# mLSTM cell and squared-ReLU FFN on one core: the front of the kernel laid in another order

## Chip, core and metric

One NeuronCore of a Trainium2 chip runs the whole kernel. The metric is the device time of one launch in microseconds (us). TensorE does the matrix products, VectorE and ScalarE (and GpSimd) the elementwise work, and the queue of SyncE (SP) issues nearly all DMAs. Each engine takes its instructions in order; engines wait for each other through semaphores.

## What is computed

```
# q, k, v, o_gate: (4, 8, 768, 40); i_gate, f_gate: (4, 8, 768)
for t in range(S):
    m_new = max(f[t] + m, i[t])
    C = exp(f[t] + m - m_new) * C + exp(i[t] - m_new) * outer(v[t], k[t])
    n = exp(f[t] + m - m_new) * n + exp(i[t] - m_new) * k[t]
    y[t] = sigmoid(o[t]) * (C @ q[t]) / max(abs(n @ q[t]), 1)
    m = m_new
x = y as (3072, 320)                  # 8 heads of 40 side by side
out = max(x @ w_in, 0) ** 2 @ w_out   # w_in (320, 2048), w_out (2048, 320), stored as 64-bit floats
```

## The kernel before

**Chunks.** The recurrence is done in chunks of 128 steps: 4 batches of 6 chunks, s = 0 to 23, all 8 heads of a chunk together. Two chunks make a group g of 256 tokens, on which the FFN works. A chunk passes through these helpers:

- The gates (`do_gates`, L251, VectorE): a max-plus scan along all 768 steps for m, and a masked sum for A, the log decay since the chunk's start. Both are 32 rows (batch and head) by 768. `turn_gates` (L263) transposes them on TensorE, and ScalarE makes the bias b_T and the factor eA_T of them.
- `transposes(s)` (L411) turns k and q into kT and qT, `scores(s)` (L422) multiplies them on TensorE.
- The decay matrix comes to the 128 partitions in one of two ways. For chunks 0 and 1, `spread_A` (L346) makes it on TensorE: one fp32 matmul of the identity with the causal mask `later` per bank (L354), and one matmul per head that selects the row of A (L358). For all later chunks A goes to memory (`a_rows`, L916) and comes back by a broadcast load, `load_A` (L337, tile A_bc, 512 KB); GpSimd puts the mask on it (`mask`, L364, L367).
- `weigh(s)` (L379) is one ScalarE exponential per head (L391), and `values(s)` (L398) on GpSimd makes the weighted values vw. `weighted(s)` (L434) multiplies scores and weights on VectorE.
- `attend(s)` (L446): on TensorE hi (queries with the state C, L453), dC (L460) and hp (this chunk's part, L467); on VectorE the decay of hi (L473) and the mask on dC (L478); on GpSimd the update of C (L481, L486).
- `normalise(s)` (L585) makes x on VectorE (L589 to L599), `turn_rows(s)` (L624) transposes it on TensorE (L629), and ScalarE copies it (L630).

**FFN.** A group has four quarters pp. `ffn1_main` (L640) is 8 matmuls 256 tokens wide (L651) into two PSUM banks; `ffn1_rest` (L657, L662) adds the last 64 of the 320 inputs, from the weights w_in2; `relu_half` and `square_half` follow on ScalarE. Everything is fp32; an fp32 matmul shows as two records in the profile.

**Weights.** w_in and w_out come as 64-bit words and are turned to fp32 on the chip, piece by piece (18 pieces; 0, 1, 3, 4, 5, 6, 8, 9 are w_in, 2 and 7 are w_in2, the rest w_out). `fetch` loads a piece into one of four raw buffers; `words` (L195) is two ScalarE instructions (L202, L204); `join` (L207) is three VectorE instructions (L213, L217, L218) and one add on GpSimd (L222), after which it fetches the piece four further on. `step` does words and join.

**Order.** The kernel is under a manual schedule: each engine runs its instructions in the order in which the program text issues them. The front is the list from L896 to L955; then a loop of u = 0 to 7 (L959) takes chunks 2 to 5 and the first FFN quarters, and a longer loop (L1031) takes the rest. `NEXT` (L958) says how many pieces are joined by the end of each u. `idle(n)` (L880) is n bf16 matmuls of zeros, 128x512, on TensorE. PSUM is in three pools: ps_at (3 banks), ps_h (3), ps_o (2). `mask(2)` stands on GpSimd ahead of the update of C by chunk 1 and of the later joins (L941, L942, L946).

Of the kernel before, what the change touches and what calls it, by code (L numbers as in the profile page):

```python
# [17 lines left out]
P = 128  # L18
# [11 lines left out]
def kernel(  # L30
# [60 lines left out]
    conv = brought.enter_context(tc.tile_pool(name="conv", bufs=2, side="right"))  # L91

# [18 lines left out]
    later = gates.tile([P, P], F32)  # L111

# [4 lines left out]
    def make_consts():  # L117
# [4 lines left out]
        for t in va_w:  # L122
# [4 lines left out]

        nc.gpsimd.memset(sel[:], 0.0)
        nc.gpsimd.affine_select(
            sel[:], sel[:], compare_op=ALU.not_equal, fill=1.0, base=0, pattern=[[-1, H], [0, P]], channel_multiplier=1,  # L130
        )

        nc.gpsimd.memset(later[:], 0.0)
        nc.gpsimd.affine_select(
            later[:], later[:], compare_op=ALU.is_ge, fill=-1e30, base=0, pattern=[[1, P]], channel_multiplier=-1,
# [111 lines left out]
    def load_gates():  # L247
        nc.sync.dma_start(f_sb[:], f_gate.rearrange("b h s -> (b h) s"))
        nc.scalar.dma_start(i_sb[:], i_gate.rearrange("b h s -> (b h) s"))

    def do_gates():  # L251
        nc.vector.tensor_tensor_scan(m_sb[:], f_sb[:], i_sb[:], -1e30, op0=ALU.add, op1=ALU.max)
        nc.vector.memset(f_sb[:, 0:1], 0.0)
        nc.vector.tensor_tensor(f_sb[:, 1:], f_sb[:, 1:], m_sb[:, : S - 1], op=ALU.add)
        nc.vector.tensor_tensor(f_sb[:, 1:], f_sb[:, 1:], m_sb[:, 1:], op=ALU.subtract)
        nc.vector.tensor_scalar_max(f_sb[:], f_sb[:], LOG_ZERO)
        nc.vector.tensor_tensor_scan(
            A_sb[:], keep[:].rearrange("p c t -> p (c t)"), f_sb[:], 0.0, op0=ALU.mult, op1=ALU.add,
        )
        nc.vector.tensor_tensor(i_sb[:], i_sb[:], m_sb[:], op=ALU.subtract)  # L260
        nc.vector.tensor_tensor(i_sb[:], i_sb[:], A_sb[:], op=ALU.subtract)

    def turn_gates():  # L263
        for src, dst in ((i_sb, b_T), (A_sb, eA_T)):
            tp = ps_o.tile([P, W], F32, name="tp", tag="o_ps")[:, : S // P * BH].rearrange("p (c r) -> p c r", r=BH)
            for c in range(NB):
                nc.tensor.transpose(tp[:, c, :], src[:, c * P : (c + 1) * P], ident[:BH, :BH])
            nc.scalar.activation(
                dst[:].rearrange("p b c h -> p c b h"), tp.rearrange("p c (b h) -> p c b h", b=B),
                AF.Copy if dst is b_T else AF.Exp,  # L270
            )
# [74 lines left out]
    def spread_A(s):  # L346

        b, c = divmod(s, NB)
        H2 = H // 2
        d = st.setdefault(s, {})  # L350
        d["A"] = []
        for i in range(2):
            A = ps_h.tile([P, H2, P], F32, name="A_ps", tag="h_ps")
            nc.tensor.matmul(  # L354
                A[:], lhsT=ident[:], rhs=later[:].unsqueeze(1).to_broadcast([P, H2, P]), start=True, stop=False,
            )
            for h in range(H2):
                nc.tensor.matmul(  # L358
                    A[:, h, :], lhsT=sel[:, i * H2 + h, :], rhs=A_sb[:, c * P : (c + 1) * P],
                    start=False, stop=(h == H2 - 1),  # L360
                )
            d["A"].append(A)
# [16 lines left out]
    def weigh(s, masked=False):  # L379
        b, c = divmod(s, NB)  # L380
        d = st[s]
        A, n = d["A"], H // len(d["A"])
        d["W"] = flat_c[:, H * P * (s % 2) : H * P * (s % 2 + 1)].rearrange("p (h t) -> p h t", t=P) if s < W_IN else A[0]
        if s < X_SQ:
            d["dec"] = prep.tile([P, H], F32, name="dec")
        if len(A) == 1 and not masked:
            mask(s)
        for i in range(len(A)):
            hh = slice(i * n, (i + 1) * n)
            for h in range(n):  # L390
                nc.scalar.activation(  # L391
                    d["W"][:, i * n + h, :], A[i][:, h, :], AF.Exp, bias=b_T[:, b, c, i * n + h : i * n + h + 1],
                )
            if s < X_SQ:
                nc.scalar.activation(d["dec"][:, hh], A[i][:, :, P - 1], AF.Exp)
        values(s)
# [14 lines left out]
    def transposes(s, o=(False, False)):  # L411
        d = st[s]
        kqT(s)
        for i, n in enumerate(("kT", "qT")):
# [5 lines left out]
            (nc.scalar.copy if i == 0 or s in (0, *range(2, 7)) else nc.vector.tensor_copy)(d[n], tp)  # L420
# [25 lines left out]
    def attend(s):  # L446
        b, c = divmod(s, NB)
        d = st[s]
        C = st.get("C")
        if c > 0:  # L450
            hi = ps_at.tile([P, H, D1], F32, name="hi", tag="at")
            for j in range(PR):
                nc.tensor.matmul(  # L453
                    hi[:, 2 * j : 2 * j + 2, :].rearrange("p h d -> p (h d)"), lhsT=d["qT"][:, j, :],
                    rhs=C[:, j].rearrange("p h d -> p (h d)"), start=True, stop=True,
                )
        if c + 1 < NB:
            dC = ps_at.tile([P, PR, 2, D1], F32, name="dC", tag="at")
# [6 lines left out]
        hp = d["hp"] = ps_at.tile([P, H, D1], F32, name="hp", tag="at")  # L465
        for h in range(H):
            nc.tensor.matmul(  # L467
                hp[:, h, :], lhsT=d["P"][h % 2][:, h // 2, :], rhs=d["va"][:, h, :], start=True, stop=True,
            )
        d["num"] = hp  # L470
        if c > 0:
            num = d["num"] = old.tile([P, H, D1], F32, name="num", bufs=1)
            nc.vector.tensor_tensor(  # L473
                num[:], hi[:], eA_T[:, b, c, :].unsqueeze(2).to_broadcast([P, H, D1]), op=ALU.mult,
            )
        if c + 1 < NB:
            Cn = old.tile([P, PR, 2, D1], F32, name="C_sb")
            nc.vector.tensor_tensor(Cn[:], dC[:], bdm[:], op=ALU.mult)  # L478
            if c > 0:
                Cd = old.tile([P, H, D1], F32, name="Cd", bufs=1)  # L480
                nc.gpsimd.tensor_tensor(  # L481
                    Cd[:], C[:].rearrange("p j i d -> p (j i) d"),
# [4 lines left out]
            st["C"] = Cn  # L487

# [96 lines left out]
    def normalise(s):  # L585
# [4 lines left out]
        dm = work.tile([P, H], F32, name="dm")  # L590
# [3 lines left out]

        x = d["x"] = work.tile([P, 3 * P], F32, name="x_sb")
        x3 = x[:, :DM].rearrange("p (h d) -> p h d", d=D)
        nc.vector.tensor_tensor(x3, num[:, :, :D], d["og"], op=ALU.mult)
        nc.vector.tensor_tensor(x3, x3, dm[:].unsqueeze(2).to_broadcast([P, H, D]), op=ALU.mult)
        nc.vector.tensor_copy(x[:, DM:], x[:, DM - KR : DM])  # L599

# [39 lines left out]
    def ffn1_main(g, pp):  # L640

        if pp == 0:
            new_g2(g)
        xT = st["xT", g]

        hs = [ps_h.tile([P, 2, WG], F32, name="h_ps") for _ in range(2)]
        for i in range(2):
            for n in range(2):
                fb = 4 * pp + 2 * n + i
                for a in range(2):  # L650
                    nc.tensor.matmul(  # L651
                        hs[i][:, n, :], lhsT=w_in[:, a, fb * P : (fb + 1) * P], rhs=xT[:, :, a, :],
                        start=(n == 0 and a == 0), stop=False,
# [242 lines left out]
    load_gates()  # L896
    load_part(0, 0)
    load_part(0, 1)
    fetch(2)
    make_consts()  # L900
    load_part(1, 0)
    load_part(1, 1)
    load_part(0, 2)
    fetch(1)
    load_o(0)
    load_o(1)
    load_part(1, 2)
# [3 lines left out]
    idle(4)  # L911
    scores(0)
    idle(3)
    do_gates()
    rounding.words()
    nc.scalar.dma_start(A_d[:, :], A_sb[:])  # L916
    spread_A(0)
    rounding.words()
    turn_gates()
    rounding.join()  # L920
    weigh(0)
    transposes(1, (False, True))
    spread_A(1)
    scores(1, (True, True))
    weigh(1)
    first.close()
    ffn = ctx.enter_context(tc.tile_pool(name="ffn", bufs=2))
# [218 lines left out]
```

## Time and profile before

| | us |
|---|---|
| Median of 3 runs (513.91 to 514.52) | 514.11 |
| Profiled execution, own time | 512.99 |
| Its span | 511.2 |
| TensorE busy in it | 502.6 |
| VectorE busy | 347.0 |
| ScalarE busy | 248.7 |
| GpSimd busy | 112.7 |
| Mean granted TensorE clock | 0.997 of full |

Times in a timeline count from the span's start. A line has the start, the length, the engine (PE is TensorE, DVE VectorE, ACT ScalarE, POOL GpSimd), the source line, the operation, output<-inputs by the program's names, the shape, the number of instructions put together in the line, and in brackets how long the engine was idle before and what ended that. Lengths of overlapping instructions add up to more than the distance of their starts, so a cost per instruction is better read from start to start. A busy TensorE isn't one at its peak.

### The profile page before, as it was taken

What the parts mean: (1) busy time and instruction counts of PE and PEld (TensorE: products, weight loads), DVE (VectorE), ACT (ScalarE), POOL (GpSimd) and SP (SyncE); (2) the same over time, 40 slices, a digit from 0 to 9 for tenths busy, and PEclk for the clock granted to TensorE, in tenths of its full rate; (3) what the DMA queues carried; (4) which work ended last, traced back from release to release, by engine and by line L of the source; (5) the groups of instructions that cost most, each with busy time, mean ns of one, the idle gap of its engine ahead of it and who ended that gap; (6) DMA issues with size and microseconds to landing.
All of it is one profiled execution on the core that took longest, in us unless ns stands there. A gap on an engine that the chain in (4) does not pass through costs nothing.

```text
span 511.2 us, 11842 instructions
## 1 busy us (share of the span) xinstructions
PE 502.6 (98%) x4648; PEld 460.9 (90%) x4649; DVE 347.0 (68%) x630; ACT 248.7 (49%) x492; POOL 112.7 (22%) x138
## 2 busy tenths in 40 slices
PE   9999999999999999999999999999999999999997
PEld 4878888787798999999999999999999999999997
DVE  8588966564879767667768777667768666644341
ACT  3768798654440650770660870560861650432400
POOL 3356733312022121112112130122112121020000
PEclk9998999999999999999999999999999999999999
DMA  9999899855675786675675786685655352100000
GB/s 191 207 237 220 246 234 207 135 121 106 115 168 98 167 159 128 153 161 115 158 151 113 172 158 117 161 165 101 165 122 116 94 120 79 46 10 25 0 27 27
DMA packets 238231, 67.63 MB, mean 132 GB/s; under 512 B 185600, under 2 KB 232704, under 8 KB 238176
## 3 DMA queue, kind: packets, MB, share of 16 engines
q1 hardware_dynamic: 238080, 66.68, 61.6%
q8 instruction: 37, 0.61, 0.5%
q10 hardware_dynamic: 96, 0.20, 0.1%
q14 instruction: 18, 0.15, 0.1%
HBM read 54.56 MB, written 17.86 MB: 142 GB/s over the span
## 4 chain that ended last, share of the span: by engine, by line
PE 85%; DVE 8%; ACT 2%; issue 2%; DMA 2%; SPq 1%; POOL 0%; DVEq 0%; POOLq 0%; ACTq 0%
PE h_ps L742 32%; PE h_ps L816 21%; PE h_ps L848 7%; PE h_ps L651 6%; PE tp L429 4%; PE h_ps L688 3%; PE numT L528 3%; PE numT L519 2%; PE h_ps L662 2%; DVE mag L217 2%; PE hp L467 1%; DMA A_bc<-a_rows 1%; PE A_ps L358 1%; PE dC L538 1%; ACT g_c L391 1%
## 5 line engine op out<-in xcount | busy, mean ns | idle before, releaser
L367 POOL TENSOR_SCALAR_AFFINE_SELECT A_bc<-A_bc 128x1024 f32<-128x1024 f32 x22 | 25.5, 1161 | 215.0 <-ACT kq L377 170.0
L742 PE MATMUL h_ps<-T,S 128*128 128x160 f32 x352 | 51.4, 299 | 0.0
L742 PE MATMUL h_ps<-w_out,g 128*128 128x160 f32 x336 | 49.2, 303 | 0.0
L742 PEld LDWEIGHTS h_ps<-T,S 128*128 128x128 f32 x352 | 49.0, 190 | 0.0
L377 ACT ACTIVATE kq<-A_bc 64x512 f32<-64x512 f32 x30 | 18.9, 630 | 61.1 <-DMA A_bc<-a_rows 60.8
L391 ACT ACTIVATE A_bc<-A_bc,b_T 128x128 f32<-128x128 f32 x144 | 44.3, 391 | 8.4 <-POOL A_bc L367 7.9
L742 PEld LDWEIGHTS h_ps<-w_out,g 128*128 128x128 f32 x336 | 46.1, 190 | 1.1
L651 PE MATMUL h_ps<-xT,w_in 128*128 128x256 f32 x192 | 44.5, 386 | 1.6 <-ACT xT L630 1.6
L651 PEld LDWEIGHTS h_ps<-xT,w_in 128*128 128x128 f32 x192 | 36.1, 193 | 7.3 <-ACT xT L630 2.0
L829 ACT COPY r_sb<-h_ps 128x512 f32<-128x512 f32 x18 | 10.5, 586 | 63.8 <-PE h_ps L816 63.8
L816 PE MATMUL h_ps<-xT,w_in 128*128 128x128 f32 x288 | 40.7, 284 | 0.4 <-ACT r_sb L829 0.4
L758 DVE TENSOR_TENSOR y_sb<-y_sb,h_ps 128x160 f32<-128x160 f32 x44 | 14.1, 320 | 36.7 <-PE h_ps L742 36.6
L816 PE MATMUL h_ps<-xs,w_in 128*128 128x128 f32 x288 | 38.0, 275 | 0.0
L816 PEld LDWEIGHTS h_ps<-xT,w_in 128*128 128x128 f32 x288 | 34.9, 191 | 3.4 <-ACT r_sb L829 0.6
L848 PE MATMUL h_ps<-xT,w_in 64*128 64x128 f32 x432 | 36.9, 280 | 0.0
L848 PEld LDWEIGHTS h_ps<-xT,w_in 64*128 64x128 f32 x432 | 33.4, 187 | 2.2
L816 PE MATMUL h_ps<-xs,WS 128*128 128x128 f32 x288 | 35.1, 275 | 0.0
L816 PEld LDWEIGHTS h_ps<-xs,w_in 128*128 128x128 f32 x288 | 35.1, 192 | 0.0
L816 PEld LDWEIGHTS h_ps<-xs,WS 128*128 128x128 f32 x288 | 33.6, 192 | 0.0
L545 DVE STREAM_TRANSPOSE tn<-numT 128x256 f32<-128x256 f32 x36 | 15.9, 449 | 21.2 <-PE numT L528 21.2
L853 DVE TENSOR_TENSOR r_sb<-r_sb,h_ps 128x512 f32<-128x512 f32 x18 | 12.4, 686 | 25.7 <-PE h_ps L848 25.6
L444 DVE TENSOR_TENSOR A_bc<-tp,A_bc 128x512 f32<-128x512 f32 x36 | 23.1, 684 | 9.5 <-PE tp L429 9.5
(168 smaller groups left out, 1069.9 us busy)
## 6 DMA issues: line engine op xcount, KB each, us to landing
A_bc<-a_rows SPq DMA_DIRECT2D x22, 512.0 KB, 4.6
raw<-in_moe_w_out_dram SPq DMA_DIRECT2D x8, 640.0 KB, 4.7
num_rows<-tn SPq DMA_DIRECT2D x18, 256.0 KB, 3.0
kq<-num_rows SPq DMA_DIRECT2D x72, 64.0 KB, 2.6
kqT<-kq_rows SPq DMA_DIRECT2D x34, 128.0 KB, 3.2
raw<-in_moe_w_in_dram SPq DMA_DIRECT2D x8, 512.0 KB, 5.9
kq<-in_k_dram SPq DMA_DIRECT2D x24, 160.0 KB, 4.9
va<-in_v_dram SPq DMA_DIRECT2D x24, 160.0 KB, 5.2
```

The costliest lines, as they stand in the source:

```text
L367: nc.gpsimd.affine_select(A[:], A[:], compare_op=ALU.is_ge, fill=-1e30, base=0, pattern=[[0, H], [1, P]], channel_multiplier=-1,)
L377: nc.scalar.activation(e[rows], st[s]["A"][0][rows, PR * i : PR * (i + 1), :], AF.Exp)
L391: nc.scalar.activation(d["W"][:, i * n + h, :], A[i][:, h, :], AF.Exp, bias=b_T[:, b, c, i * n + h : i * n + h + 1],)
L429: nc.tensor.matmul(sc[i][:, j, :], lhsT=d["kT"][rows, j, :], rhs=d["qT"][rows, j, :], start=True, stop=True,)
L444: nc.vector.tensor_tensor(t, d["sc"][i], d["W"][:, heads, :], op=ALU.mult)
L528: nc.tensor.matmul(numT[i][halves[g], e, :], lhsT=va_w[s % NKQ][:, h * D1 : h * D1 + DP], rhs=d["P"][h % 2][:, h // 2, :] if s < KQ_SQ els ...
L545: nc.vector.transpose(to[:, 2 * i : 2 * i + 2], numT[i][:, :2, :].rearrange("p c t -> p (c t)"))
L651: nc.tensor.matmul(hs[i][:, n, :], lhsT=w_in[:, a, fb * P : (fb + 1) * P], rhs=xT[:, :, a, :], start=(n == 0 and a == 0), stop=False,)
L688: nc.tensor.matmul(o_ps, lhsT=st["g2", g][:, fb, j * P : (j + 1) * P], rhs=w_out[:, fb, :], start=(fb == 0), stop=(fb == NF - 1),)
L742: nc.tensor.matmul(to, lhsT=lhsT[:, p], rhs=rhs[:, p, :], start=(start and p == 0), stop=(p == NPAIR - 1), skip_group_check=True,)
L816: nc.tensor.matmul(to[:, n, :], lhsT=lhsT[:, 4 * q + n, :], rhs=rhs, start=(start and n == 0), stop=True, skip_group_check=True,)
L848: nc.tensor.matmul(to[:, n, :], lhsT=w_in2[rows, 4 * q + n, :], rhs=rhs, start=False, stop=True, skip_group_check=True,)
```

## The change

- The gates are done in two parts: the first two chunks (256 steps), then the other four. Each part has its own loads (`load_gates(part)`), `gates_floor`, `gates_sum` and `turn_gates`. The arithmetic is reordered: f - i, plus the m before, clamped from both sides, gives the log decay, and its part above zero plus A gives minus b, whose sign the copy to b_T turns.
- `spread_A` is split: `spread_mask` puts the mask into both banks by bf16 matmuls (identity and mask are copied to bf16 on VectorE); bank i holds the heads of parity i.
- `weigh` can do the first or second half of its heads alone; `ffn1_main` can do one chunk (128 tokens) alone; `attend` is cut into `from_C`, `to_C`, `from_chunk`, `decayed`, `next_C`, and `normalise` into `denominators` and `gated`. Calls that aren't in the front keep the order within them, but hp's matmuls go even heads first.
- `transposes` copies both tiles on ScalarE (before, qT of chunk 1 went to VectorE).
- The order of loads: k and q of chunk 2 come into the first list, the values behind the keys and queries, raw pieces later.
- The front is in a new order, with fewer idle matmuls (15 of 27 remain). Chunk 2's scores, both halves of the first FFN quarter and the transposes of chunk 3 come before the loop. In the loop, u = 0 has chunk 3's weights only, and at u = 1 ffn1(0,1) stands ahead of attend(2); at u = 2 turn_rows(2) comes after ffn1(0,2).

The diff, cut; the bodies of `from_C` to `next_C` and of `denominators` and `gated` are those of `attend` and `normalise`:

```diff
+        nc.gpsimd.memset(later[:], 0.0)
+        nc.gpsimd.affine_select(
+            later[:], later[:], compare_op=ALU.is_ge, fill=-1e30, base=0, pattern=[[1, P]], channel_multiplier=-1,
+        )
+        nc.vector.tensor_copy(ident_h[:], ident[:])
+        nc.vector.tensor_copy(later_h[:], later[:])
...
+    FIRST = 2
+    SPANS = (slice(0, FIRST * P), slice(FIRST * P, S))
...
+    def gates_floor(part):
+        cols = SPANS[part]
+        c0, c1 = cols.start, cols.stop
+        tt = nc.vector.tensor_tensor
         nc.vector.tensor_tensor_scan(
+            m_sb[:, cols], f_sb[:, cols], i_sb[:, cols], -1e30 if c0 == 0 else m_sb[:, c0 - 1 : c0],
+            op0=ALU.add, op1=ALU.max,
         )
+        g = i_sb
+        tt(g[:, cols], f_sb[:, cols], i_sb[:, cols], op=ALU.subtract)
+        if c0 == 0:
+            nc.vector.memset(g[:, 0:1], 0.0)
+        a = max(c0, 1)
+        tt(g[:, a:c1], g[:, a:c1], m_sb[:, a - 1 : c1 - 1], op=ALU.add)
+        nc.vector.tensor_scalar(f_sb[:, cols], g[:, cols], scalar1=0.0, scalar2=LOG_ZERO, op0=ALU.min, op1=ALU.max)
+
+    def gates_sum(part):
+        cols = SPANS[part]
+        nc.vector.tensor_tensor_scan(
+            A_sb[:, cols], keep[:].rearrange("p c t -> p (c t)")[:, cols], f_sb[:, cols], 0.0, op0=ALU.mult, op1=ALU.add,
+        )
+        nc.vector.scalar_tensor_tensor(
+            i_sb[:, cols], in0=i_sb[:, cols], scalar=0.0, in1=A_sb[:, cols], op0=ALU.max, op1=ALU.add,
+        )
...
+    def spread_mask(s):
+
+        d = st.setdefault(s, {})
+        d["A"] = [ps_h.tile([P, PR, P], F32, name="A_ps", tag="h_ps") for _ in range(2)]
+        for A in d["A"]:
+            nc.tensor.matmul(
+                A[:], lhsT=ident_h[:], rhs=later_h[:].unsqueeze(1).to_broadcast([P, PR, P]), start=True, stop=False,
+            )
...
-    def weigh(s, masked=False):
+    def weigh(s, masked=False, part=None):
...
-            (nc.scalar.copy if i == 0 or s in (0, *range(2, 7)) else nc.vector.tensor_copy)(d[n], tp)
+            nc.scalar.copy(d[n], tp)
...
-    def ffn1_main(g, pp):
+    def ffn1_main(g, pp, half=None):
...
+        js = slice(0, GT) if half is None else slice(half, half + 1)
+        cols = slice(js.start * P, js.stop * P)
...
-                        hs[i][:, n, :], lhsT=w_in[:, a, fb * P : (fb + 1) * P], rhs=xT[:, :, a, :],
-                        start=(n == 0 and a == 0), stop=False,
+                        hs[i][:, n, cols], lhsT=w_in[:, a, fb * P : (fb + 1) * P], rhs=xT[:, js, a, :],
+                        start=(n == 0 and a == 0 and not half), stop=False,
...
-    load_gates()
+    load_gates(0)
     load_part(0, 0)
     load_part(0, 1)
-    fetch(2)
+    load_gates(1)
     make_consts()
+    load_part(0, 2)
     load_part(1, 0)
     load_part(1, 1)
-    load_part(0, 2)
     fetch(1)
     load_o(0)
+    load_part(1, 2)
+    fetch(1)
     load_o(1)
-    load_part(1, 2)
+    fetch(1)
+    load_part(2, 0)
+    load_part(2, 1)
     fetch(1)
     idle(12)
     transposes(0)
-    idle(4)
+    spread_mask(0)
+    idle(3)
+    gates_floor(0)
+    gates_sum(0)
+    spread_A(0, 0)
+    turn_gates(0)
+    spread_A(0, 1)
     scores(0)
-    idle(3)
-    do_gates()
+    weigh(0)
+    gates_floor(1)
+    weighted(0)
+    gates_sum(1)
     rounding.words()
+    transposes(1, (True, True))
+    spread_mask(1)
+    for i in range(2):
+        spread_A(1, i)
+    weigh(1, part=0)
     nc.scalar.dma_start(A_d[:, :], A_sb[:])
-    spread_A(0)
+    weigh(1, part=1)
+    rounding.join()
+    from_chunk(0)
+    to_C(0)
+    denominators(0)
+    next_C(0)
+    scores(1, (True, True))
     rounding.words()
-    turn_gates()
+    sigmoid(0)
+    sigmoid(1)
+    rounding.words()
     rounding.join()
-    weigh(0)
-    transposes(1, (False, True))
-    spread_A(1)
-    scores(1, (True, True))
-    weigh(1)
-    first.close()
-    ffn = ctx.enter_context(tc.tile_pool(name="ffn", bufs=2))
-    before = ExitStack()
-    old = before.enter_context(tc.tile_pool(name="old", bufs=2))
-    weighted(0)
     weighted(1)
-    load(2)
+    load_part(2, 2)
     load_A(2)
     load_o(2)
     load_o(3)
-    sigmoid(0)
-    sigmoid(1)
-    attend(0)
-    rounding.step()
-    normalise(0)
+    to_C(1)
+    from_C(1)
+    turn_gates(1)
+    first.close()
+    ffn = ctx.enter_context(tc.tile_pool(name="ffn", bufs=2))
+    from_chunk(1)
+    gated(0)
+    decayed(1)
+    turn_rows(0)
     mask(2)
-    attend(1)
+    transposes(2)
     normalise(1)
+    next_C(1)
+    ffn1_main(0, 0, 0)
+    rounding.words()
+    turn_rows(1)
     load(3)
     load_A(3)
-    rounding.step()
-    turn_rows(0)
-    idle(4)
-    transposes(2)
-    idle(4)
+    rounding.join()
+    rounding.words()
+    scores(2)
+    ffn1_main(0, 0, 1)
+    ffn1_rest(0, 0, st["half"][0])
+    rounding.join()
+    weigh(2, masked=True, part=0)
+    relu_half()
+    weigh(2, masked=True, part=1)
+    transposes(3, (True, True))
+    rounding.join()
+    weighted(2)
     sigmoid(2)
     sigmoid(3)
-    turn_rows(1)
-    weigh(2, masked=True)
-    rounding.step()
...
     for u in range(8):
         s = 2 + u // 2
         relu_half()
-        if u % 2 == 0:
-            if u == 0:
-                ffn1(0, 0)
-                scores(s)
-                rounding.step()
-            else:
+        if u == 0:
+            weigh(3)
+            rounding.words()
+            square_half()
+        elif u % 2 == 0:
+            if u > 2:
                 turn_rows(s - 1)
-                scores(s)
-                ffn1(u // 4, u % 4)
+            scores(s)
+            ffn1(u // 4, u % 4)
             if u == 2:
+                turn_rows(s - 1)
                 rounding.words()
             weighted(s)
...
+            if u == 1:
+                ffn1(0, 1)
             attend(s)
...
-            transposes(s + 1)
+            if u > 1:
+                transposes(s + 1)
             rounding.words()
-            ffn1(u // 4, u % 4)
+            if u > 1:
+                ffn1(u // 4, u % 4)
             square_half()
```

## The prediction

> **What bounds the kernel now.** I read first the page's busy shares, then the timelines of TensorE, GpSimd and VectorE over the first 70 us (the change ends there), then the DMA answer for the first 50 us.
>
> The page's first rows, engine busy shares and the forty slices:
> ```profile
> PE 502.6 (98%) x4648; PEld 460.9 (90%) x4649; DVE 347.0 (68%) x630; ACT 248.7 (49%) x492; POOL 112.7 (22%) x138
> PE   9999999999999999999999999999999999999997
> ```
> TensorE has no hole in any slice, so after the front a delay or a lead of TensorE is carried to the end. I therefore ask one thing: at what time does TensorE reach the first step that is the same in both kernels? That is turn_rows(3), the transposes of chunk 3's x, at 64.92 before.
>
> TensorE before, around the first FFN matmuls (start, length, instruction, wait):
> ```profile
> 27.23 0.82 PE L883 MATMUL idle<-zeros 128*128 128x512 bf16 x3
> 31.25 3.72 PE L651 MATMUL h_ps<-xT,w_in 128*128 128x256 f32 x16 [0.57 <-ACT xT L630]
> 34.90 1.14 PE L662 MATMUL h_ps<-xT,w_in 64*128 64x256 f32 x8
> 43.81 4.12 PE L651 MATMUL h_ps<-xT,w_in 128*128 128x256 f32 x16
> 50.49 3.72 PE L651 MATMUL h_ps<-xT,w_in 128*128 128x256 f32 x16
> 64.92 0.52 PE L629 MATMUL tp<-ident,x_sb 128*128 128x128 f32 x3 [0.52 <-DVE x_sb L598]
> ```
> The FFN quarters (0,0), (0,1), (0,2) start at 31.25, 43.81 and 50.49. At 64.92 TensorE waits for VectorE, so VectorE is level with it there.
>
> GpSimd before, in its program order:
> ```profile
> 27.96 1.35 POOL L367 TENSOR_SCALAR_AFFINE_SELECT A_bc<-A_bc 128x1024 f32<-128x1024 f32 x1 [2.84 <-DMA A_bc<-a_rows]
> 29.28 0.97 POOL L481 TENSOR_TENSOR Cd<-C_sb,dec 128x328 f32<-128x328 f32 x1
> 30.33 1.04 POOL L486 TENSOR_TENSOR C_sb<-C_sb,Cd 128x328 f32<-128x328 f32 x1
> 32.52 1.32 POOL L222 TENSOR_TENSOR w_in<-mag,low 128x512 int32<-128x512 int32 x1 [1.15 <-DVE mag L218]
> ```
> mask(2) cannot start before A_bc of chunk 2 lands (27.9); C's update and the weights' final add stand behind it.
>
> The DMA answer for 0 to 50 us:
> ```profile
> DMA  0499999999999989896989699999999689999996
> q1 hardware_dynamic: 27262, 10.39, 102.1%
> A_bc<-a_rows SPq DMA_DIRECT2D x3, 512.0 KB, 5.8
> ```
> From 3 us to 50 us SP's queue never runs dry: what lands when is set by the bytes queued ahead, not by when a load is asked for.
>
> **What the notes say.** (1) The Trainium skill, DMA: Bandwidth & Descriptors, Queues, rings and completion order: on each DMA engine descriptors are consumed in ring order. The trace agrees: loads land in the order of issue, 4.8 to 8 us after it. (2) The Trainium skill, GPSIMD Engine Reference, Specifications: GpSimd's SBUF interfaces are shared with VectorE, which contends when it has two SBUF inputs or runs a 2-port mode. The trace agrees: L217 takes 0.43 us alone (22.61) and 1.38 beside L222 (32.75). (3) The Trainium skill, TensorE: Matmul & The Clock Gate, Part 1: after an idle window of about 3.4 us the array runs at half rate. The trace is harsher: TensorE has nothing from about 38.0 to 39.1, and the windows show a granted clock of 0.50 at 42 to 44 us.
>
> **The change part by part.**
>
> *Gates in two parts.* VectorE before: 4.12 to 10.19 for A. A 768-wide scan takes 1.74, so 256 columns take (1.74-0.06)/3+0.06 = 0.62; a subtract or add 0.35, the clamp 0.22. Two scans, two tensor_tensor, a clamp: 2.3 us with gaps. VectorE is free at 3.9 (memsets to 3.50, two new copies to bf16 at an estimated 0.2). The loads of a third of the bytes are then there (whole ones: 3.7 and 4.1). A for chunks 0 and 1 is ready at 6.2, 4.0 us sooner.
>
> *Masks in bf16.* L354 takes 1.02 us per bank in fp32. The same shape in bf16 is L883: four from 28.76 to 29.71, 0.24 each. Four masks: 4 x 0.78 = 3.1 us off TensorE. Idle matmuls: 12 of 27 go, about 2.6 us. The price of the half-width FFN: eight 128-wide matmul records of L816 take 0.99, so 16 take 1.98, twice that is 3.96 against 3.65: +0.3.
>
> *ScalarE.* sigmoid(0,1) and sigmoid(2,3) are now split by exponentials: two more table loads of 1.28. The copy of chunk 1's qT moves to ScalarE (0.6). Cover: ScalarE is idle 3.45 us at 37.4 to 40.8 before.
>
> *The front's gain.* weigh(0) runs from 9.1 instead of 14.51: gates turned at 8.5, behind the idle(3) and one spread_A of 1.08. Then ScalarE: 2.2 for weigh(0), 1.15 words, 1.1 copies, 2.4 for weigh(1): done at 16.0 (20.6 before). VectorE: gates_floor(1), weighted(0), gates_sum(1) to 13.9; join of piece 0 to 15.5; then piece 1, which meets GpSimd's add of piece 0, to 19.1; weighted(1) to 20.4 (21.8 before). TensorE: hp(1) 20.9 to 22.6, turn_rows(0) to 23.1, transposes(2) to 24.1, the half FFN on chunk 0 24.1 to 26.1, turn_rows(1), scores(2), the half on chunk 1 27.7 to 29.7. Before, this work (L651 and scores(2)) is done at about 36.0. So at 29.7 TensorE leads by 6.3 us.
>
> *Where the lead ends.* The next step, ffn1_rest(0,0), needs piece 2 of the weights (w_in2), whose add on GpSimd is queued behind mask(2) and C's update, as before. But the load of A_bc(2) now stands behind one more transfer: raw piece 5, 512 KB, issued by the join of piece 1 ahead of it (before: raw 5 came after). At the rate of this stretch that is 1.6 us (2.15 between landings before). Nothing else ahead of it changes by more than a few tenths, so A_bc(2) lands at about 27.9+1.6-0.2 = 29.3, although its issue comes sooner. GpSimd sits idle from 20.4 to then. From there one chain, each link in program order on its engine:
> - mask, Cd, add: 3.4 (27.96 to 31.37): 32.7. Piece 2: 1.3: 34.0.
> - ffn1_rest 1.05: 35.1. relu_half stands between the halves of weigh(2) on ScalarE: 1.05 + 1.25: 37.4. vw(2) 0.8: 38.2. Piece 4, queued behind vw(2): 1.3: 39.5.
> - ffn1(0,1) 4.85, now ahead of attend(2): 44.3. hi(2) 0.95: 45.3.
> - VectorE has waited since 38.7 (weighted(2)): decay and C 1.4, join of piece 5 1.8, normalise(2) 2.7 with contention, join of piece 6 1.6: 52.8. Add on GpSimd 1.3: 54.1.
> - ffn1(0,2) starts at 54.1 (before 50.49) and takes 4.8; turn_rows(2) 0.5: 59.4. Attend(3) starts there, 55.21 before.
>
> The lead of 6.3 us has become a lag of 4.2. The words of piece 9 stand behind turn_rows(2)'s copy on ScalarE (60.1), so the join of piece 9, attend(3)'s VectorE part and the join of piece 10 follow: x of chunk 3 near 69.3, against 65.0: **+4.3 us**.
>
> *The clock.* TensorE stalls at 29.7 to 34, 36 to 39.5 and 49 to 54. One 1.1 us stall before cost a stretch of 3.4 us at half rate, 1.7 us of work. Bounds: 0 (the stretch falls into the next stall, and before has one too) to three hits, 1.05 for ffn1_rest and 1.7 each for (0,1) and (0,2): 4.5. I take one, **+1.7**.
>
> Sum against the profiled execution's own 512.99 (span 511.2 and 1.8 around it): 512.99+4.3+1.7 = 519.0. The median of the runs is 1.1 higher: 514.1+6.0 = **520.1**.
>
> **The rivals.**
> - *A_bc(2) lands early (not slower).* The chain above gives equality when ffn1(0,2) starts 0.5 before turn_rows(2)'s old place, that is when ffn1(0,1) starts at 36.9, so A_bc(2) at 26.7 decides. For it: A's write to memory is issued near 14.9 only, but its load right after join 1, and a transfer may overtake. Against: the full queue. At 24.5 the chain starts 4.8 sooner, the stalls shrink and no half clock comes (before pays about 1.3): 512.
> - *TensorE's work alone counts.* It is at 98%; 3.1+2.6-0.3 = 5.4 us less work would end at 508.7, if GpSimd and VectorE kept pace. Against it: VectorE would have to stand ready with pieces 5 to 7 at 45, with two holes of 7 us ahead.
> - *Every stall halves the clock.* +4.3+4.5: 522.9, up to 525 if A_bc(2) is later still.
> - *A wash.* Joins that fall into holes of GpSimd are 0.95 shorter (1.38 against 0.43 for L217). If four more than I allow are short and the clock holds: 514.1+4.3-3.8 = 514.6.
>
> **How the numbers follow.** A measurement of this kernel can tell about 0.2% (1 us) from no change. Forecast, 515.2 to 522: 0.50. Half clock at every stall, above 522: 0.17. Wash: 0.08. Early landing, 510.5 to 513: 0.13. TensorE's work alone, below 510.5: 0.12. Slower 0.67, same 0.08, faster 0.25. The range leaves out the lowest case and what lies above 524.5: 511.0 to 524.5. The forecast's own range is 515.2 to 522.
>
> **What would show it.** GpSimd idle for some 8 us ahead of mask(2), released by the DMA of A_bc near 29; TensorE waiting before L662's line for w_in2 on GpSimd; VectorE idle before hi(2) for over 4 us; ffn1(0,2) later than 50.5; a granted clock of 0.5 somewhere between 30 and 60 us. If mask(2) starts before 26.7, the prediction is wrong.

## The result, and the profile after

| | before | after |
|---|---|---|
| Median (before 513.91 to 514.52; after 528.71 to 530.68, 4 runs) | 514.26 | 529.12 |
| Ratio, 95% interval | | 1.0295 (1.0273 to 1.0317) |
| Profiled execution, its own time | 512.99 | 530.68 |
| Its span | 511.2 | 528.8 |
| Mean granted TensorE clock | 0.997 | 0.961 |

Slower, as forecast, but by 14.9 us where 6.0 were forecast, and above the range (511.0 to 524.5). Of some kernels below, one or two runs lie over 1.5% above the fastest; the ratios leave these out, the medians do not. The page of the kernel after, in its first rows and the row of granted clock:

```profile
PE 512.7 (97%) x4649; PEld 471.8 (89%) x4649; DVE 343.0 (65%) x636; ACT 250.8 (47%) x497; POOL 111.3 (21%) x138
PE   9997689999999999999999999999999999999997
...
PEclk9668697999999999999999999999999999999999
```

A slice is 13.2 us. TensorE now has holes in slices 4 to 6, as the chain of the prediction said, and five of the first seven slices show a clock below 9. Slice 2 (13 to 26 us) has a busy digit of 9 and a clock digit of 6: TensorE works without a pause and is slow. The same in stretches of 10 us, first before, then after; the third number from the right (PEclk) is the granted clock:

```profile
core 0: us, PE busy (x) PEld busy (x) DVE busy (x) ACT busy (x) POOL busy (x), PEclk, DMA share, GB/s
20.00:30.00 10.00, 9.95 (x84) 8.68 (x83) 8.73 (x21) 6.97 (x16) 4.06 (x4) 1.00 0.90 207
50.00:60.00 10.00, 10.00 (x78) 8.78 (x75) 9.79 (x14) 8.20 (x20) 6.54 (x7) 1.00 0.74 233
```
```profile
20.00:30.00 10.00, 10.00 (x57) 9.56 (x57) 4.63 (x10) 3.82 (x8) 2.44 (x3) 0.50 1.03 256
50.00:60.00 10.00, 6.50 (x56) 5.21 (x52) 7.62 (x16) 5.91 (x10) 3.24 (x5) 0.78 0.27 69
```

Both are fully busy from 20 to 30 us, but where before has 84 matmul records, after has 57 (not all of the same work), at a clock of 0.50. In stretches of 1 us the profiled run after is at half rate at 11.2 (for 3.4 us), 18.1 (17.1), 45.4 (3.4), 55.6 (10.2) and 79.5 (6.8): 41 us. Before has one stretch of 3.4 (both have some again in the last microsecond).

TensorE after, around the first FFN matmuls:

```profile
38.96 1.14 PE L719 MATMUL h_ps<-xT,w_in 64*128 64x256 f32 x8
44.46 4.98 PE L708 MATMUL h_ps<-xT,w_in 128*128 128x256 f32 x14 [2.90 <-POOL w_in L228]
61.14 5.60 PE L708 MATMUL h_ps<-xT,w_in 128*128 128x256 f32 x14 [3.34 <-POOL w_in L228]
80.10 0.87 PE L684 MATMUL tp<-ident,x_sb 128*128 128x128 f32 x3 [2.76 <-DVE x_sb L649]
```

ffn1_rest(0,0) starts at 38.96 (34.90 before), ffn1(0,1) waits for its weights until 44.46 (43.81), ffn1(0,2) until 61.14 (50.49), and turn_rows(3), where the prediction measured, is at 80.10 (64.92): 15.2 later, of the 17.7 by which this execution is longer. The rest comes just behind it, where the last stretch of half rate lies (79.5 to 86.3): turn_rows(4) is 18.1 later (98.42 for 80.29). ffn1_rest(0,0) isn't held by its weights here, whose add ends at 36.2; TensorE itself gets there only at 38.96. GpSimd and VectorE after:

```profile
28.83 1.09 POOL L396 TENSOR_SCALAR_AFFINE_SELECT A_bc<-A_bc 128x1024 f32<-128x1024 f32 x1 [5.51 <-DMA A_bc<-a_rows]
29.89 0.74 POOL L523 TENSOR_TENSOR Cd<-C_sb,dec 128x328 f32<-128x328 f32 x1
32.84 0.94 POOL L528 TENSOR_TENSOR C_sb<-C_sb,Cd 128x328 f32<-128x328 f32 x1 [2.21 <-DVE C_sb L520]
34.93 1.31 POOL L228 TENSOR_TENSOR w_in<-mag,low 128x512 int32<-128x512 int32 x1 [1.16 <-DVE mag L224]
```
```profile
30.02 0.50 DVE L638 TENSOR_TENSOR num<-num,hp 128x328 f32<-128x328 f32 x1 [4.06 <-PE hp L502]
32.20 0.49 DVE L520 TENSOR_TENSOR C_sb<-dC,bdm 128x328 f32<-128x328 f32 x1
51.58 0.50 DVE L511 TENSOR_TENSOR num<-hi,eA_T 128x328 f32<-128x328 f32 x1 [8.19 <-PE hi L481]
```

mask(2) is released by the load of A_bc at 28.8 after 5.5 us of idleness, as predicted (29.3). But behind it the add to C waits 2.2 us more for VectorE's masked dC (L520). On VectorE that stands behind normalise(1), which waits 4.1 us for hp(1) (L638), done only at 29.8 on a TensorE at half rate. The load was the last link in the plan; at half rate TensorE is.

### The profile page after: what moved, and what is told of

It is laid out like the page before. It is cut to its first block, busy times and chain, and to the rows that moved or that the text cites. A ratio compares the mean times of both kernels' runs of the same rounds, so it can differ in the third digit from the quotient of the medians.

```text
span 528.8 us, 11861 instructions
## 1 busy us (share of the span) xinstructions
PE 512.7 (97%) x4649; PEld 471.8 (89%) x4649; DVE 343.0 (65%) x636; ACT 250.8 (47%) x497; POOL 111.3 (21%) x138
## 4 chain that ended last, share of the span: by engine, by line
PE 89%; DVE 5%; issue 2%; POOL 1%; ACT 1%; DMA 1%; SPq 0%; POOLq 0%; DVEq 0%
PE h_ps L799 31%; PE h_ps L873 21%; PE h_ps L708 8%; PE h_ps L905 7%; PE tp L459 4%; PE numT L577 3%; PE h_ps L745 3%; PE h_ps L719 2%; PE numT L568 2%; PE hp L502 2%; PE dC L491 1%; DVE mag L223 1%; PE hi L481 1%; PE dC L587 1%; PE A_ps L388 1%
## 5 line engine op out<-in xcount | busy, mean ns | idle before, releaser
L708 PE MATMUL h_ps<-xT,w_in 128*128 128x256 f32 (+1 forms) x208 | 52.5, 412 | 8.6 <-POOL w_in L228 7.5
L708 PEld LDWEIGHTS h_ps<-xT,w_in 128*128 128x128 f32 x208 | 41.8, 221 | 16.7 <-POOL w_in L228 8.9
L815 DVE TENSOR_TENSOR y_sb<-y_sb,h_ps 128x160 f32<-128x160 f32 x44 | 14.0, 318 | 37.6 <-PE h_ps L799 37.6
L873 PEld LDWEIGHTS h_ps<-xT,w_in 128*128 128x128 f32 x288 | 34.9, 191 | 2.8 <-issue 0.5
L910 DVE TENSOR_TENSOR r_sb<-r_sb,h_ps 128x512 f32<-128x512 f32 x18 | 12.4, 687 | 25.7 <-PE h_ps L905 25.5
```

Of the source, the lines that this page charges most:

```text
L708: nc.tensor.matmul(hs[i][:, n, cols], lhsT=w_in[:, a, fb * P : (fb + 1) * P], rhs=xT[:, js, a, :], start=(n == 0 and a == 0 and not half), ...
L873: nc.tensor.matmul(to[:, n, :], lhsT=lhsT[:, 4 * q + n, :], rhs=rhs, start=(start and n == 0), stop=True, skip_group_check=True,)
```

## The experiments

Two theories. **Order**: the waits of the new order make up the loss, whatever the clock. **Clock**: a large part is TensorE at half rate, either because of its empty stretches or because of what it is given to do in the front. Where kernels of different groups are compared, it is by their ratios to the kernel before. Idle matmuls are zeros in bf16 whose product nobody reads; those in front of a mask are overwritten by it.

**1. Idle matmuls all through the new front; none at all in the old one.**

```diff
# after_warm: 33 more, idle(3) behind scores(0), spread_A(1, *), to_C(0), scores(1),
# from_C(1), from_chunk(1), transposes(2), and
     transposes(3, (True, True))
+    idle(12)
# before_cold: the three idle(4) of the front out
-    idle(4)
```

Expected of after_warm:

> The changed kernel with 33 more idle matmuls (seven groups of 3 in the front, 12 ahead of ffn1(0,1)). Clock theory (the thin matmuls and the missing fillers let the granted clock fall to half, and half-rate work on TensorE is most of the loss): the half-rate time falls from 34 to 41 us to under 14 us, hp(1) ends near 24 instead of 30, and the time is 516 to 521 us. Order theory (the waits of the new order on GpSimd and VectorE are the loss): the fillers add work, 528 to 533 us. A further point for either: with a full clock mask(2), released by A_bc at about 29, is the link that comes last ahead of the first ffn1_rest.

Expected of before_cold:

> The kernel before without its three idle(4) groups (one after transposes(0), two about transposes(2)); 12+3 idle matmuls remain, as in the changed kernel. Clock theory: half-rate stretches appear in the first 35 us, 517 to 523 us. Order theory: nothing was lost with them, 512 to 514.5 us.

after_warm 524.45, ratio 1.019 (1.0166 to 1.0215): about 5 us come back, with 20.5 us at half rate in the profiled run: between the two ranges, for more than the 14 us expected stay at half rate. before_cold 514.45, 0.9989 (0.9969 to 1.0009), no difference, where the clock theory asked for 517 to 523: it has 10 us at half rate and the time doesn't show it. So activity in the new front counts, and in the old front the idle matmuls are no gain or loss.

**2. The bf16 masks alone, in the kernel before.**

```diff
-                A[:], lhsT=ident[:], rhs=later[:].unsqueeze(1).to_broadcast([P, H2, P]),
+                A[:], lhsT=ident_h[:], rhs=later_h[:].unsqueeze(1).to_broadcast([P, H2, P]),
```

Expected of before_bf16:

> The kernel before with the two masks of spread_A made by bf16 matmuls, nothing else changed. Work-counts theory: 3.1 us less on TensorE in the front, 511 to 512 us. Clock theory: the fp32 masks were also what kept the array busy between thin matmuls, so one or two half-rate stretches take the gain back: 513 to 518 us.

522.1, 1.015 (1.0118 to 1.0182): four matmul instructions made four times shorter cost 7.3 us or more, above the ranges of both theories. TensorE in this kernel:

```profile
16.01 2.07 PE L362 MATMUL A_ps<-A_sb,sel 32*128 32x128 f32 x8
18.02 0.61 PE L358 MATMUL A_ps<-later_h,ident_h 128*128 128x512 bf16 x1
18.55 2.07 PE L362 MATMUL A_ps<-A_sb,sel 32*128 32x128 f32 x8
...
24.35 3.55 PE L471 MATMUL hp<-va,g_c 128*128 128x41 f32 x16
```

Its stretch from 20 to 30 us, with the clock third from the right:

```profile
20.00:30.00 10.00, 10.00 (x54) 9.55 (x54) 5.16 (x13) 5.55 (x12) 3.98 (x4) 0.50 0.97 194
```

The same matmuls before:

```profile
16.06 1.15 PE L358 MATMUL A_ps<-A_sb,sel 32*128 32x128 f32 x8
17.14 1.13 PE L354 MATMUL A_ps<-later,ident 128*128 128x512 f32 x2
18.20 1.15 PE L358 MATMUL A_ps<-A_sb,sel 32*128 32x128 f32 x8
...
21.33 1.92 PE L467 MATMUL hp<-va,g_c 128*128 128x41 f32 x16
```

Eight spreading matmuls take 2.07 for 1.15, hp 3.55 for 1.92: half rate from 13.4 to 37.3, and no hole in TensorE's work until 35.4. What remains at this place are thin matmuls, 32 rows deep or 41 columns wide.

**3. Is it the activity, or something else in that edit?** Three zero matmuls into the same bank ahead of each bf16 mask give TensorE back about the time of the fp32 mask; and, the other way round, fp32 masks in the kernel after.

```diff
# before_bf16_warm
+            for _ in range(3):
+                nc.tensor.matmul(
+                    A[:].rearrange("p a b -> p (a b)"), lhsT=zeros[:, :1].to_broadcast([P, P]),
+                    rhs=zeros[:, :1].to_broadcast([P, W]), start=True, stop=True,
+                )
             nc.tensor.matmul(
                 A[:], lhsT=ident_h[:], rhs=later_h[:].unsqueeze(1)
# after_fp32
-    lhsT=ident_h[:], rhs=later_h[:].unsqueeze(1)
+    lhsT=ident[:], rhs=later[:].unsqueeze(1)
```

Expected of before_bf16_warm:

> The kernel before with bf16 masks, and ahead of each mask three bf16 matmuls of zeros into the same bank, about as long as the fp32 mask was. Clock theory: the half-rate stretch of 24 us that the bf16 masks brought is gone, and the time is back at 513.5 to 516 us, although the same real work is done by the same instructions as in the bf16 kernel. If it was something else in that edit (the two copies on VectorE, the reordered constants), it stays at 520 us or more.

Expected of after_fp32:

> The changed kernel with its four masks in fp32 again, nothing else changed: 3.1 us more work on TensorE. Clock theory: less half-rate time ahead of 35 us, 522 to 527 us. Work-counts theory: 530 to 532 us.

before_bf16_warm 513.3, 0.9984 (0.9969 to 0.9998, 20 runs): the whole loss is gone, with the bf16 masks, the two copies and the moved constants still in. Zeros do as well as data. They put the thin work behind them back to its old place in time as well, so this run alone doesn't tell activity from timing; the count further below does. after_fp32 524.19, 1.0192 (1.0153 to 1.023): about 5 us back, full clock until 51.7 us.

**4. The order: ffn1(0,1) behind attend(2), as in the kernel before; the same with fillers; and a filler in the one empty stretch of the kernel before.**

```diff
# after_u1 (after_warm_u1: with the edit of after_warm too)
+            attend(s)
             if u == 1:
                 ffn1(0, 1)
-            attend(s)
# before_fill, u = 0
                 scores(s)
+                idle(4)
```

Expected of after_u1:

> The changed kernel with attend(2) ahead of ffn1(0,1) at u=1 again. Order theory: VectorE's 8.2 us wait for hi(2) shrinks by some 5 us, the joins of pieces 5 to 7 come sooner and ffn1(0,2) starts near 56 instead of 61: 522 to 525 us. Clock theory: TensorE is at half rate up to 35 us either way, so at most 2 to 4 us come back: 525 to 528 us.

Expected of after_warm_u1:

> The changed kernel with the 33 idle matmuls of the warm run and attend(2) ahead of ffn1(0,1) at u=1. If the clock and the order are two separate losses, the two gains (4.7 and 3.3 us) add up: 520 to 522 us. If both were one and the same lost time, no more than 1 us comes on top of the warm run: 523 to 525 us.

Expected of before_fill:

> The kernel before with idle(4) behind scores(2) at u=0, where TensorE has a hole of 1.1 us behind hi(2) (it waits there for VectorE). Clock theory: the hole is filled, the one half-rate stretch of before (41.4 to 44.8) does not come, TensorE gains up to 1.3 us there, of which VectorE, nearly level with it, lets some through: 512.5 to 514 us. Otherwise no change, 514 to 515 us.

after_u1 525.81, 1.0226 (1.02 to 1.0253): some 3.5 back. after_warm_u1 523.64, 1.0189 (1.0145 to 1.0233): 5.4, not 3.5 + 5.4, as if both were one loss. Its trace shows why the order brings nothing more here: with ffn1(0,1) out of the way, VectorE next waits for the words of pieces on ScalarE (4.0 us for those behind weigh(3), 2.9 later on). before_fill 513.03, 0.999 (0.9977 to 1.0003): full clock throughout, but its stretch of half rate cost the kernel before no more than this measurement tells.

**5. The places of two sets of words and of the load of A_bc(2), with fp32 masks.**

```diff
# w9, u = 2
-                turn_rows(s - 1)
                 rounding.words()
+                turn_rows(s - 1)
# abc
+    load_part(2, 2)
+    load_A(2)
     rounding.join()
     weighted(1)
-    load_part(2, 2)
-    load_A(2)
# order: w9, after_u1 and
-            weigh(3)
             rounding.words()
+            weigh(3)
# all: order and abc
```

Expected of after_fp32_w9:

> The changed kernel with fp32 masks (full clock up to 52 us), and at u=2 the words of piece 9 ahead of turn_rows(2)'s copy on ScalarE. The prediction had the path from attend(3) to turn_rows(3) 2.1 us too short (9.9 against 12.0 measured in the fp32 run), and the words of piece 9 wait for the end of ffn1(0,2) there. If that is the mis-sized term: VectorE's 3.5 us wait for mag goes, x of chunk 3 comes 2 to 3.5 us sooner, 520.5 to 522.5 us. If another wait takes its place (the joins behind it were bound by GpSimd): 523.5 to 524.5.

Expected of after_fp32_abc:

> The changed kernel with fp32 masks, and the loads of chunk 2's values and of A_bc(2) ahead of raw piece 5. If the prediction's first link holds, A_bc(2) lands about 1.6 us sooner (27 instead of 28.7), mask(2), piece 2 and ffn1_rest(0,0) follow, and all of it reaches the end: 522 to 523 us. If piece 2 is then bound by its own join on VectorE, less than 1 us.

Expected of after_fp32_order:

> The changed kernel with fp32 masks, attend(2) ahead of ffn1(0,1), the words of piece 5 ahead of weigh(3) and those of piece 9 ahead of turn_rows(2). Order theory: VectorE no longer waits for hi(2) (6.5 us) or for mag (3.5); pieces 5 to 7 are joined by 48 instead of 54, ffn1(0,2) starts near 49, attend(3) near 54 (55.2 in the kernel before): 512 to 516 us. If the new front has lost time by something else than the clock and these orders, it stays above 518.

Expected of after_fp32_all:

> The same as the order run, with chunk 2's values and A_bc(2) loaded ahead of raw piece 5: about 1 us less than that run, 511 to 515 us; it would be the first with this front not slower than the kernel before.

The first two can't be read as tests of their edits: after_fp32_w9 529.42, 1.0292 (1.026 to 1.0324), fell back to half rate at 18.2 for 17.1 us, although it differs from after_fp32 only at u = 2, some 40 us later. So did after_fp32_abc, 528.36, 1.024 (1.0189 to 1.0291); its one run at a clock of 0.987, where after_fp32 runs, took 522.14 against 524, and one run is no test. A_bc did land earlier there (26.3 for 28.9), and GpSimd then waited 6.3 us for VectorE's dC in TensorE's slow stretch. after_fp32_order 518.47, 1.0095 (1.0065 to 1.0125): the three moves of order give 5 us back, and 512 to 516 had been expected. after_fp32_all 521.04, 1.0131 (1.0093 to 1.0169), no better, where 511 to 515 were expected; its runs go from 516.3 (clock 0.990) to 523.9 (0.974).

**6. The price of the order and of the clock apart.** after_order has the order of after_fp32_order with bf16 masks. after_fp32_warm leaves the order and holds the clock with fillers; all_warm is after_fp32_all with fillers, all_warm_sig has the sigmoids of chunks 2 and 3 moved as well.

```diff
# after_fp32_warm: fp32 masks, idle(3) behind to_C(0), scores(1), from_C(1), from_chunk(1), and
+    idle(4)     # ahead of ffn1_rest(0, 0)
+    idle(12)    # ahead of ffn1(0, 1)
+    idle(16)    # ahead of ffn1(0, 2)
+    idle(8)     # ahead of turn_rows(3)
# all_warm: the same with 4, 8, 6 in the last three; all_warm_sig: and
-    sigmoid(2)
-    sigmoid(3)
             rounding.words()
             weigh(3)
+            sigmoid(2)
+            sigmoid(3)
```

Expected of after_fp32_warm:

> The changed kernel with fp32 masks, 16 idle matmuls spread over the front (four groups of 3 and one of 4) and 12, 16 and 8 more in TensorE's holes ahead of ffn1(0,1), ffn1(0,2) and turn_rows(3); its order is untouched. It asks what the new order costs when the clock stays full. By the prediction's own sum 4.3 us: 518.5. By the fp32 run, whose turn_rows(3) came 8.1 us later than before with the clock full up to 52 us: 520 to 522. If 523 or more, a part of the loss is neither the clock nor these waits.

Expected of after_order:

> The changed kernel with its bf16 masks, attend(2) ahead of ffn1(0,1), and the words of pieces 5 and 9 ahead of weigh(3) and turn_rows(2): the order mended, the clock left to itself. If order and clock are separate losses, some 5 to 6 us come back and the half-rate stretch of the front stays: 522 to 525 us. If mending the order is enough to keep the clock: 516 to 519.

Expected of all_warm:

> The changed kernel with fp32 masks, the mended order, A_bc(2) ahead of raw piece 5, and idle matmuls in the thin stretch of the front and in the holes left in that order (4, 8 and 6). With the clock full throughout, the mended order should show its own time: the run of the same order without the idle matmuls had turn_rows(3) at 69.7 with half-rate stretches at 12 to 15 and 49.5 to 56 us in it, some 3 us of work: 511 to 515 us. If the new front's gain on VectorE is real, it is below 513; if the fillers only replace half-rate time, 516 or more.

Expected of all_warm_sig:

> The same, and the two sigmoids of chunks 2 and 3 behind weigh(3) instead of ahead of it, so that ScalarE reaches weigh(3) without two table loads and two sigmoids in between (3.4 us). If ScalarE's late weigh(3) is what holds weighted(3) and piece 7, 0.5 to 2 us less than the run without that move; if the pieces' joins on VectorE hold them, the same.

after_fp32_warm 521.7, 1.016 (1.0126 to 1.0195); its profiled run, at a clock of 1.000, took 520.39. after_order 520.49, 1.017 (1.0117 to 1.0224), between its two ranges, at a clock of 0.964 to 0.977: the order can be mended without the clock. all_warm 523.48, 1.0187 (1.0165 to 1.0209), with half rate at 17.8 for 10.2 us in spite of the fillers (511 to 515 expected). all_warm_sig 518.32, 1.0072 (1.0047 to 1.0097); its runs at a clock of 1.0 took 517.0 to 517.4. All of all_warm's runs are at 0.987 to 0.990, so the two don't tell what the move of the sigmoids is worth. The best version of the new front is still 3 to 4 us slower than before (513.96; 513.06 in its run at a clock of 1.0).

The fillers of after_fp32_warm moved ffn1_rest(0,0) 1.9 us (35.59 for 33.71), so the last two put them only where TensorE waits: 10 ahead of ffn1(0,1) (left out in fp32_holes2), 14 ahead of ffn1(0,2), 7 ahead of turn_rows(3).

```diff
# after_fp32, and
+    idle(10)    # not in fp32_holes2
+    idle(14)
+    idle(7)
```

Expected of fp32_holes:

> The new front with fp32 masks and its order untouched, with bf16 matmuls of zeros only inside TensorE's own waits (10 ahead of ffn1(0,1), 14 ahead of ffn1(0,2), 7 ahead of turn_rows(3)), so that they should delay nothing: ffn1_rest(0,0) near 33.7, ffn1(0,1) near 39.2, ffn1(0,2) near 54.2, as with fp32 masks alone. If the order alone costs what the prediction said plus the two waits found after attend(3) (4.3 + 1.3 + 1.3, less overlap), the time at full clock is 518 to 519, turn_rows(3) near 70.5 to 71. If the order costs the whole 7.4 that the run with more idle matmuls showed, it is 520 to 521 with turn_rows(3) near 72.8. If the clock falls back all the same, 522 to 524 and nothing is told apart.

Expected of fp32_holes2:

> The same without the 10 ahead of ffn1(0,1). If an empty stretch of TensorE is enough to bring half rate, the 2.8 us ahead of ffn1(0,1) bring one stretch near 39 to 43 and 1 to 1.5 us more than with them filled; if not, the two kernels are within 0.5 us.

fp32_holes 523.38, 1.0189 (1.0164 to 1.0214): half rate again, from 20.5 to 34.2, in a part of the program that it shares with fp32_holes2. fp32_holes2 522.0, 1.0185 (1.0144 to 1.0227); its profiled run took 520.27 at the clock of before (0.997, one stretch of 3.4 us at 55). The gap of 2.8 us that it leaves empty at 36.4 brought no half rate: the expectation that an empty wait is enough failed. Two of its stretches, one in the gap and one behind it, then its TensorE and VectorE:

```profile
37.00:38.00 1.00, 0.00 (x0) 0.00 (x0) 1.00 (x2) 1.00 (x4) 0.80 (x2) 1.00 1.03 260
41.00:42.00 1.00, 1.00 (x6) 0.87 (x6) 0.00 (x0) 0.99 (x3) 0.00 (x0) 1.00 1.09 263
```
```profile
33.71 1.13 PE L719 MATMUL h_ps<-xT,w_in 64*128 64x256 f32 x8 [1.20 <-POOL w_in L228]
39.22 3.29 PE L708 MATMUL h_ps<-xT,w_in 128*128 128x256 f32 x14 [2.78 <-POOL w_in L228]
43.50 1.12 PE L481 MATMUL hi<-C_sb,kqT 128*128 128x82 f32 x8
54.22 4.98 PE L708 MATMUL h_ps<-xT,w_in 128*128 128x256 f32 x14 [1.88 <-POOL w_in L228]
60.57 1.02 PE L481 MATMUL hi<-C_sb,kqT 128*128 128x82 f32 x8
72.56 0.52 PE L684 MATMUL tp<-ident,x_sb 128*128 128x128 f32 x3 [1.15 <-DVE x_sb L649]
```
```profile
61.85 0.43 DVE L219 TENSOR_SCALAR mag<-mag 128x512 f32<-128x512 f32 x1 [3.03 <-ACT mag L208]
65.61 1.02 DVE L219 TENSOR_SCALAR mag<-mag 128x640 f32<-128x640 f32 x1 [1.33 <-POOL vw L433]
66.67 1.06 DVE L223 TENSOR_SCALAR mag<-mag 128x640 int32<-128x640 int32 x1
69.03 1.29 DVE L640 TENSOR_SCALAR dm<-num 128x8 f32<-128x8 f32 x1
71.15 1.26 DVE L649 TENSOR_TENSOR x_sb<-x_sb,dm 128x320 f32<-128x320 f32 x1
```

The first four TensorE starts are the prediction's 34.0, 39.5, 44.3 and 54.1 within 0.8 us; the last two are not its 59.4 and 69.3.

## Why the prediction was right in direction and wrong in size

The sum of the prediction was 519.0 for the profiled execution, which took 530.68: 11.7 too little. fp32_holes2 divides it. With the order of the change, and through fp32 masks and 21 fillers nearly the clock of before, it takes 520.27, so some 1.3 belong to the order and 530.68 - 520.27 = 10.4 to the clock and what it drags. The division is that of two profiled runs; by the ratios to the kernel before (1.0295 and 1.0185) the clock's share is some 6 us, because the other runs of after have a clock of 0.968 and those of fp32_holes2 mostly 0.993.

- **The clock, the step that failed.** The prediction took one stretch, +1.7, with three (4.5) as its bound, because it let half rate follow only from TensorE's stalls. Measured: 41 us of it, 20.5 before the first stall. The step behind it is "3.1 us off TensorE" for the bf16 masks, which the prediction counted as a gain of the front and nowhere as a risk to the clock: taken alone that edit costs 7.3 us or more, and zeros in the freed time take the loss away. The size of the work was right, what it does to the time was not: the fp32 masks had kept TensorE's clock up in a stretch of thin matmuls. The rival "every stall halves the clock" asked for too little as well (522.9 to 525), and for the wrong reason: fp32_holes2 keeps full rate across an empty 2.8 us, and the kernel after loses it without a hole.
- **The lead of 6.3 us by 29.7.** It never came about in the kernel after: hp(1) is done at 29.8 where 22.6 was planned. With fp32 masks it is done at 25.5, against 26.7 before, so the clock took most of the lead; the 2.9 us that are missing there with fp32 masks are about the 3.1 of these masks themselves. Two small terms of the front were off too: the copies to bf16 take 0.71 and 0.47 us where 0.2 were allowed, and A is ready at 6.8 for 6.2.
- **A_bc(2) as the last link.** Its landing was right (28.8 for 29.3), and so was the reading of SP's queue: mask(2) waits for it with GpSimd idle. (The time from issue to landing in that queue, given as 4.8 to 8 us, is 2.9 to 7.9 in the trace before; the sum doesn't rest on it.) In the kernel after, VectorE's masked dC of chunk 1 comes later still, through half rate. At full clock the load is the last link again (fp32_holes2: C's update follows the mask with no wait).
- **The chain from there to ffn1(0,2).** Right at full clock, link by link (54.22 for 54.1), VectorE's wait for hi(2) included (6.5 us for 6.6). after_u1, and the order of after_fp32_order, confirm that these waits carry time: 3.5 and 5 us.
- **From attend(3) to turn_rows(3).** 9.9 us planned, 12.0 measured. attend(3) is 1.2 late, through the one stretch at half rate which the prediction had entered apart. Then three terms were small: the join of piece 10, a piece 640 wide, takes 2.9 beside GpSimd instead of about 1.6; VectorE waits 1.33 until GpSimd's vw is done ahead of it; normalise takes 4.0 instead of 2.7, two of its instructions 1.3 each. Less the +1.7 already in the sum, 72.56 is 1.6 later than planned, about the 1.3 at the end.
- **"TensorE's work alone counts"** and **"A_bc(2) lands early"**: neither came. With the order mended and the clock full the new front takes 517.0 to 517.4, not 508.7; bringing A_bc forward alone moved GpSimd's wait to VectorE's masked dC, in a kernel at half rate.

**What decides when the clock falls.** Stretches come in steps of 3.4 us (3.4, 6.8, 10.2, 17.1, 23.9), and one kernel's runs differ (after_fp32_abc 0.974 to 0.987). The Trainium skill, TensorE: Matmul & The Clock Gate, Part 1, says that the window in which activity is watched is free-running, about 3.4 us long, and that the same kernel so varies from run to run; these runs agree. Its table ties half rate to an idle window, and there they differ: from 7.7 to 11.1 the kernel after runs matmuls without a hole, and is at half rate from 11.2.

```profile
7.71 1.15 PE L388 MATMUL A_ps<-A_sb,sel 32*128 32x128 f32 x8
8.70 0.25 PE L292 MATMUL tp<-ident,i_sb 32*128 32x32 f32 x2
8.79 0.28 PE L292 MATMUL tp<-ident,A_sb 32*128 32x32 f32 x2
8.92 1.13 PE L388 MATMUL A_ps<-A_sb,sel 32*128 32x128 f32 x8
9.98 1.16 PE L459 MATMUL tp<-kqT 40*128 40x128 f32 x16
11.07 1.84 PE L447 MATMUL tp<-ident,kq 128*128 128x128 f32 x8
```

A count over the traces shows what these matmuls lack. In each trace the changes of the clock lie on one grid of 3.41 us, which gives the windows. For each window, add up the columns of TensorE's matmul records, each times its rows out of 128 (the first number of 32*128 in its line), an fp32 record twice (a 128x512 record takes 0.51 us in fp32, 0.24 in bf16). Of the 3,000 windows of the 20 traces, from 4 us on, every one that counts under 3,020 is followed by half rate (91), every one over 3,120 by full rate (2,897), and 12 between go either way. The window of the lines above, 7.8 to 11.2, counts 2,596: eight spreading records bring only 512 in 1.1 us, while the 16 records of a 256-wide FFN quarter bring 8,192 in 3.7. Without the rows the count doesn't separate: the same window would then hold 8,566, more than many that keep the clock.

- An fp32 mask counts 2,048, a bf16 one 512, three matmuls of zeros and a bf16 mask 2,048 again: that is experiments 2 and 3. before_bf16 falls behind a window of 2,090.
- The kernel before stands near the edge: its window from 10.7 counts 3,060 and keeps the clock, that of before_cold from 10.8 counts 3,049 and loses it. Its 1.1 us hole lies in a window of 2,359; the 2.8 us gap of fp32_holes2 is shared by two windows of 3,654 and 4,546.
- fp32_holes falls at 20.5 behind a window of 2,856. In fp32_holes2 the eight idle matmuls from 2.61 on take 2.44 us instead of 3.62, the work behind them lies some 0.9 us earlier, and up to 51 us no window counts under 3,167: the same program, cut by its windows at other places.
- At half rate work takes twice as long, so a window holds less of it (hp: 3.55 us for 1,312, instead of 1.92). A stretch of thin matmuls so keeps itself slow until wide ones come.

**What stays open.** The count was fitted to these traces, and no run was made to test it. What sets the place of the windows in an execution isn't shown, nor why all four runs of after_fp32_w9 were slow alike. The rest of 3 to 4 us of the mended front isn't settled.

## What to carry to other kernels

Ahead of making TensorE's work shorter in a stretch of thin matmuls, ask whether that work keeps its clock up: count columns times rows per 3.41 us, against the 3,020 to 3,120 of these traces, and test it by putting bf16 zero matmuls of the same count in its place. Read the granted clock beside the busy share for every stage: a stage that is full at half rate is a hole that the busy share hides. Compare single edits only at the same granted clock, and when an engine's lead ends at a load, follow the chain behind that load to the next step that both kernels share.

## What the runs showed of the hardware that was not expected

- Half rate while TensorE's record is full: the first 22 us of a stretch of 23.9 in before_bf16, and all 17.1 of one in after. Matmuls of zeros held the full rate as well as data.
- What goes with the clock in these traces is the work of the 3.41 us before, columns times rows (under 3,020 half rate, over 3,120 full rate), not whether TensorE is busy.
- A whole idle gap of 2.8 us at full rate (fp32_holes2), where one of 1.1 us was followed by half rate in the kernel before: what counted was the work of the 3.41 us window about it (two of 3,654 and 4,546 against one of 2,359).
- A kernel that differs only at 60 us has a fall at 18 us in its trace (after_fp32_w9), and a clock of 0.968 to 0.974 in all four of its runs, where all four of after_fp32 had 0.984 to 0.990.
- A microsecond at half rate cost about 0.28 us of the time (10.4 us for 37.6 more of them), less than the half that the work itself loses; part of it falls into waits (TensorE has nothing to do from 58 to 60 us, at a clock of 0.50).
